# A gated mix of a long convolution and a two-layer network on one core: stage 2 of the convolution with taps and tokens in one product on 64x32 tiles, |C| in the exponent, a half-filled chunk of features packed into one operand

## The chip, the core and the metric

The kernel runs on one core of a Trainium2 chip. The core has a matrix engine (PE, TensorE) whose weight loads (PEld) are instructions of their own beside the matmuls, a vector engine (DVE, VectorE), an activation engine (ACT, ScalarE), a general engine (POOL, GpSimd) and an engine that here only issues transfers (SP, SyncE). Each engine works through its own list of instructions in a fixed order; semaphores hold an instruction back until what it reads is there. PE writes to PSUM, from where DVE and ACT read; POOL reaches only the large memory, SBUF. The metric is the time of one execution on the device in microseconds; several runs are taken, and the median counts.

## What is computed

Input u has 2048 tokens of 640 channels. `a` is a causal convolution of each channel with its own 2048 taps, which come from 128 complex modes; `b` is a two-layer network with 1728 hidden features; a sigmoid gate per token mixes them.

```python
dt = exp(log_dt)
A = -exp(log_A_real) + 1j * A_imag
C = (C_real + 1j * C_imag) * dt[:, None]
P = exp((A * dt[:, None])[:, :, None] * pos)          # pos = 0 .. 2047
K = 2.0 * einsum("dn,dnl->dl", C, P).real             # taps
a = irfft(rfft(u, 2 * L) * rfft(K, 2 * L))[:L] + u * D_skip
g = sigmoid((u * gate_w).sum(-1, keepdims=True))
b = relu(u @ w1) @ w2
out = g * a + (1 - g) * b
```

All inputs and the output are float32. The kernel splits the operands of the network into a high and a low part of a narrower format (f32r) and adds three products: high x high, high x low, low x high. The convolution's products stay in plain f32, and each such product stands in the profile as two MATMUL instructions.

## The kernel before

**A planner writes the order.** The kernel is written as tasks, each with an engine, a queue, an estimated duration, what it depends on and which buffers it takes or uses (`Plan.add`, L121). `Plan.run` (L160) plays the tasks through once, choosing on each engine the ready task of the best rank, and emits the instructions in that order. The order is fixed when the program is built; the chip then follows it, waiting where an estimate was too short. Tasks of one queue keep their order. Nearly every instruction bears line 228, where a helper records it, so the profile is read by tile names.

**The network (FFN), `feed_forward`, L278.** The 1728 features are cut into 14 chunks of 128, of which one has only 64; the chunks are worked in three passes (`PARTS`, 5, 5 and 4 chunks), each over 8 groups `g` of 256 tokens. The half-filled chunk stands first, in pass 0. `hidden` (L396) multiplies a pair of chunks with a group's tokens into the PSUM tile `pf`: 5 slices of 128 channels x 3 products per chunk, 256 columns each; ACT makes `hh` (ReLU, high part) and DVE `hl` (low part) from it. `sums` (L442) multiplies these with w2 into two halves of 320 columns for each of two blocks of 128 tokens, 3 products per chunk, and adds them to `q`, which is kept in DRAM between passes (`part`). In pass 0 the tokens are loaded (`xs`, L334, one buffer), turned by PE (`trans`, L343) and split into `xh` and `xl`. The 64 free feature columns of the half chunk hold zeros, save one that holds gate_w, so that the gate's logits come out of the hidden product as a row (`z`, L422) and go through DRAM to `gates` (L527). FFN tasks have the lowest rank on PE (5): they fill what the other work leaves.

**Parameters, `params`, L635.** Chains of DVE and ACT operations over 128x640 make the decay, the phase step, |C| and the angle of C. |C| takes a square root and a second set of five reciprocals. Rows of phase and decay go to DRAM (`ps`, L674) and are loaded back in another shape (`load_rows`, L798, 8 chunks of 16 channels at a time). |C| is turned by PE (`cm_pe`, L755) into the tile `cm`.

**Taps, `ssm`, L765.** 40 chunks of 16 channels. For each, PE expands phases (`pg`) and exponents (`px`, `pe`), ACT makes magnitudes (`mg`, `me`) by Exp and the trigonometric factors (`sn`, `cs`) by Sin, POOL multiplies `me` by `cm` (L862), and DVE forms five products (`factors`, L874). For each pair of chunks PE sums over the modes into `pk` (`taps`, L903), DVE turns that into `kt`, POOL adds D_skip, and the taps go to DRAM (`kd`).

**Convolution, `conv`, L960.** The transform over length is factored as 64 x 32. Five blocks `i` of 128 channels; for each block:

- `stage1` (L1014): PE transforms the 64-part for taps (from `ck`) and tokens (from `ut`), 4 quarters each; DVE turns the results into `vk` (taps, two buffers, one per block) and `va` (tokens, one buffer). Tokens of the next block wait for the relay of this one, since `va` is used again.
- `stage2` (L1044), 16 steps `j`: 12 products per step on 64x64 tiles, 128 columns each: one of the taps' spectrum and two of the tokens', the second with real and imaginary part exchanged. ACT copies the taps' part to `kw`, and one DVE multiply makes both halves of the complex product `t`.
- `inv2` (L1069), 8 steps: 16 products of 64 rows, which also add the halves of the complex product; ACT copies the result into `va`.
- `relay` (L1089): 8 DVE transposes from `va` into `vk`.
- `inv1` (L1096): 4 products with `tw`; the result is multiplied by the gate. Where the network's sum is already there, DVE multiplies and adds in one instruction (`join`, L1125) and the sum goes to the output; elsewhere ACT multiplies and the result goes to DRAM, to be added later (`with_y`, L495).

The convolution's PSUM tile `pc` has three buffers of two banks. On PE the ranks are 2 for stage 2 and its inverse, 3 for the first stages.

The heart of stage 2 and its inverse:

```python
for q, v, c0 in ((2, st['K', i], 0), (0, st['A'], 0), (1, st['A'], 32)):
    for e in range(2):
        for p in range(2):
            r, h = slice(p * 64, p * 64 + 64), p ^ e
            self.E.matmul(ps[h * 64:h * 64 + 64, p, q], st['tm'][r, 2 * j + e, c0:c0 + 64],
                          v[r, 2 * j + e], start=True, stop=True)
```

Of the kernel before, what the change touches and what calls it, by code (L numbers as in the profile page):

```python
# [24 lines left out]
SPIN = 10  # L25

# [10 lines left out]
def tables():  # L37
# [8 lines left out]
    m = np.zeros((2, 2, 32, 32, 3, 32))  # L46
    n = np.zeros((2, 2, 32, 32, 2, 2, 32))
    iw = np.zeros_like(w)
    for p in range(2):
        ct, st = c[p].transpose(2, 0, 1), s[p].transpose(2, 0, 1)  # L50
        m[p, 0, :, :, 0], m[p, 0, :, :, 1] = ct, st
        m[p, 1, :, :, 0], m[p, 1, :, :, 1] = -st, ct
        m[p, :, :, :, 2] = m[p, :, :, :, 0]
        for g in range(32):
            h = p ^ (g & 1)
            ck, sk = c[p, g], s[p, g]
            re, im = np.stack([ck, -sk], axis=1), np.stack([sk, ck], axis=1)
            n[h, 0, :, g, 0], n[h, 1, :, g, 0] = re, -re
            n[h, 0, :, g, 1], n[h, 1, :, g, 1] = im, im
            iw[p, :, g // 2 * 2 + h] = w[p, :, g]  # L60

    pt, mg, me = np.zeros((16, 8, 16, 64)), np.zeros((16, 8, 16, 64)), np.zeros((16, 8, 16, 32))
    for d in range(16):
        pt[d, :2, d, :32], pt[d, :2, d, 32:], pt[d, 2:4, d, :32] = b, 32 * b + 16, 1
        mg[d, 4:6, d], me[d, 4:6, d] = 32 * slots(), b
    tg = np.concatenate([x.reshape(128, -1) for x in (pt, mg, me)], axis=1)
    f = lambda x: np.ascontiguousarray(x.astype(np.float32))
    return dict(t_g=f(tg), t_f1=f(np.tile(np.stack([f1, f1[slots()]], axis=1), (2, 1, 1))), t_w=f(iw.reshape(128, 64)),
                t_m=f(m.reshape(128, 32, 96)), t_n=f(n.reshape(128, 32, 128)))
# [30 lines left out]
class Task:  # L100
    __slots__ = ('eng', 'q', 'dur', 'fn', 'deps', 'take', 'use', 'prio', 'mode', 'lag', 'end', 'kb', 'glue', 'port')


class Plan:
# [4 lines left out]
    HOLD = 0.3  # L109

# [10 lines left out]
    def add(self, eng, q, dur, fn, deps=(), take=(), use=(), rank=5, mode=None, kb=0, port=False):  # L121
        t = Task()
        t.eng, t.q, t.dur, t.fn, t.deps, t.take, t.use, t.mode = eng, q, dur, fn, tuple(deps), take, use, mode
        t.prio, t.end, t.kb, t.lag, t.glue, t.port = rank, None, kb, self.LAG[eng], [], port
        for b in (*take, *use):
            b.users += 1
            b.left += 1
# [15 lines left out]
    def ready(self, t, depth=0):  # L143
# [10 lines left out]
        for b in t.take:  # L154
            if not b.ring.slots:
                return 1e9, False
            r = max(r, min(b.ring.slots))
        return r, known

    def run(self):  # L160
        self.free = {e: 0.0 for e in self.LAG}
        mode, dma, log = {}, 0.0, []
        heads = {k: 0 for k in self.queues}
        while True:
# [36 lines left out]
            self.free[e] = start + change + t.dur  # L201
            if t.port:

                self.free[e] += min(max(self.free['POOL'] - start, 0), t.dur)
# [45 lines left out]
class Kernel:  # L250
    def __init__(self, tc, ctx, io, out):
# [8 lines left out]
                       xt=[T([2, 128, NT, 256], f"xt{g}") for g in range(8)], z=T([16, 128], "z_"),  # L260
                       part=[[T([128, 2, D], f"part{k}_{g}") for g in range(8)] for k in range(2)], y=T([128, 16, 4 * 128], "y_"))
        keep = self.keep = ctx.enter_context(tc.tile_pool(name="keep", bufs=1))
        self.gate, self.omg = keep.tile([128, 16], F32, name="gate"), keep.tile([128, 16], F32, name="omg")
        self.ident = keep.tile([128, 128], F32, name="ident")
# [13 lines left out]
    def feed_forward(self):  # L278
# [4 lines left out]
        for n, k in dict(ws=3, wq=5, xs=1, xhl=2, q=2, bank=2, z=1).items():  # L283
            ring(n, k)
# [12 lines left out]
        def weights(p, f, two, after=()):  # L297
            f0, fn = parts[p][f]
            first = p == 0 and not two
# [3 lines left out]
            def load():  # L303
                t = self.prm.tile([128, D], F32, name="wq", bufs=5) if first else pa.tile([128, D], F32, name="ws", bufs=3)
                st['ws', key] = t
                if two:
                    if fn < 128:
                        P.memset(t[fn:], 0.0)
                    D_.dma_start(t[:fn], io['B_w2'][f0:f0 + fn, :])
                    return  # L310
                t = t.rearrange("p (k f) -> p k f", f=128)
                if fn < 128:
                    P.memset(t[:, :, fn + 1:], 0.0)
                D_.dma_start(t[:, :, :fn], io['B_w1'][:, f0:f0 + fn].rearrange("(k p) f -> p k f", p=128))
                if fn < 128:
                    D_.dma_start(t[:, :, fn:fn + 1], io['gate_w'].rearrange("(k p o) -> p k o", p=128, o=1))

            def high():
                st[key] = [pa.tile([128, D], F32R, name=f"w{1 + two}{x}{f}") for x in 'hl']
                S.copy(st[key][0], st['ws', key])  # L320

            def low():
                V.tensor_sub(st[key][1], st.pop(('ws', key)), st[key][0].bitcast(F32))
# [10 lines left out]
        def load_x(g, after=()):  # L334
            s_ = tok('xs')

            def load():
                st['xs', g] = self.xp.tile([128, 2, D], F32, name="xs")
                for h in range(2):
                    D_.dma_start(st['xs', g][64 * h:64 * h + 64], xd[h, :, 2 * g:2 * g + 2, :])  # L340
            return s_, A('SP', 'x', 1.25, load, after, take=[s_], kb=640, rank=2 if g else 0)

        def trans(g, third, src):  # L343
# [34 lines left out]
            if third == 2:  # L378
                xst[g] = A('SP', 'st', 1.25, store, X[0, g], use=[x_], kb=1280, rank=6)
# [15 lines left out]

        def hidden(p, g, i, fs):  # L396
            b_, h_ = tok('bank'), tok(f"h{i}")

            def pe(r, f, third):
                def go():  # L400
# [3 lines left out]
                    wh, wl = (w.rearrange("p (k f) -> p k f", f=128) for w in (wh, wl))  # L404
                    for k in range(2 * third, min(2 * third + 2, NT)):
                        for m, (a, b) in enumerate(((wh, xh), (wh, xl), (wl, xh))):
                            self.E.matmul(st['hb'][:, r], a[:, k], b[:, k], start=k == m == 0,
                                          stop=k == NT - 1 and m == 2)
                return go
            ts = []  # L410
            for r, f in enumerate(fs):
                (wt, w_) = W[p, f, 0]
                for third in range(3):
                    x = X[p, g] if p else X[p, g][2 * third:2 * third + 2]
                    new = r == third == 0
                    ts.append(A('PE', 'ff', 0.72 if third < 2 else 0.36, pe(r, f, third), [*wt, *x],
                                take=[b_] if new else (), use=[w_, xtok[p, g]] + ([] if new else [b_]), mode='f'))

            if p == 0 and i == 0:
                z_ = tok('z')  # L420

                def zc():  # L422
                    st['z'] = pa.tile([65, 256], F32, name="z")
                    V.tensor_copy(st['z'][64:65], st['hb', i][64:65, 0])

                def zs():
                    D_.dma_start(sc['z'][2 * g:2 * g + 2], st['z'][64:65].rearrange("o (t p) -> o t p", t=2))
                zt = A('DVE', 'ff', 0.36, zc, ts, take=[z_], use=[b_], rank=0)
                self.zst.append(A('SP', 'st', 0.62, zs, [zt], use=[z_], kb=2, rank=6))

            def high():
                st['h', i] = [pa.tile([128, len(fs), 256], F32R, name=f"h{x}{i}") for x in 'hl']
                S.activation(st['h', i][0], st['hb', i][:, :len(fs)], AF.Relu)

            def low():
                V.scalar_tensor_tensor(st['h', i][1], st['hb', i][:, :len(fs)], 0.0, st['h', i][0].bitcast(F32),
                                       op0=ALU.max, op1=ALU.subtract)
            a = A('ACT', 'ff', 0.12 + 0.2 * len(fs), high, ts, take=[h_], use=[b_], rank=0)
            b = A('DVE', 'ff', 0.08 + 0.27 * len(fs), low, [a], use=[b_, h_], rank=0)
            H[p, g, i] = (a, b), h_  # L440

        def sums(p, g, j, q_, qld):  # L442
# [8 lines left out]
            prod = [(f, *x) for f in range(n) for x in ((0, 0), (0, 1), (1, 0))]  # L451
# [3 lines left out]
            def pe(ks):  # L455
                def go():
                    if ks[0] == 0:
                        st['sb', g, j] = pb.tile([128, 320], F32, name="pf")
                    for k in ks:
                        f, x, y = prod[k]  # L460
                        self.E.matmul(st['sb', g, j], st['h', f // 2 * 2][x][:, f % 2, ts_], st["w2", p, f][y][:, ns],
                                      start=k == 0, stop=k == 3 * n - 1)
# [14 lines left out]
            ks, a = list(range(3 * n)), []  # L477
            for k in range(0, 3 * n, 4 if j == 0 else 5):
                part = ks[k:k + (4 if j == 0 else 5)]
                dep = [x for f, _, y in (prod[k] for k in part) for x in W[p, f, 1][0]]  # L480
                dep += [hs[f // 2][0][x] for f, x, _ in (prod[k] for k in part)]
# [45 lines left out]
        def gates():  # L527
            def load():
                st['zt'] = pa.tile([128, 16], F32, name="zt")
                D_.dma_start(st['zt'], sc['z'].rearrange("b p -> p b"))  # L530

            def go():
                z = st['zt']
# [7 lines left out]
            a = A('SP', 'q', 0.62, load, self.zst, kb=8, rank=3)  # L541
            rec = Recorder(V)
            for k in range(17):
                a = A('DVE', 'gate', 0.2, rec.one(k, 17, go), [a], rank=4)
            self.gated = a

        self.zst, self.x_read = [], []
# [4 lines left out]
        if SPIN:  # L552
            A('PE', 'ff', 1.7 + 0.43 * SPIN, spin, mode='f')
        xs = {0: load_x(0)}
# [682 lines left out]
```

## Time and profile before

| | |
|---|---|
| median of 3 runs | 714.4 us (713.83 to 715.64) |
| the profiled execution | 717.8 us, of which 716.0 are the span from the first to the last instruction |
| mean granted clock of PE | 0.986 |
| instructions | 21643, of which 9489 matmuls and as many weight loads |

A row of a group in the profile gives line, engine, operation, output tile <- input tiles, shape and count; then busy time in all and the mean of one in ns; then how long the engine stood idle just before them, and what ended it. Matmuls overlap in time, so their mean is a latency: what one costs is read from the distance of their starts. "issue" as a reason for a wait means that the engine waited for nothing that the profile shows. In rows of stretches, each engine's busy time is followed by its count of instructions, then PE's granted clock, the share of the transfer engines and GB/s.

### The profile page before, as it was taken

What the parts mean: (1) busy time and instruction counts of PE and PEld (TensorE: products, weight loads), DVE (VectorE), ACT (ScalarE), POOL (GpSimd) and SP (SyncE); (2) the same over time, 40 slices, a digit from 0 to 9 for tenths busy, and PEclk for the clock granted to TensorE, in tenths of its full rate; (3) what the DMA queues carried; (4) which work ended last, traced back from release to release, by engine and by line L of the source; (5) the groups of instructions that cost most, each with busy time, mean ns of one, the idle gap of its engine ahead of it and who ended that gap; (6) DMA issues with size and microseconds to landing.
All of it is one profiled execution on the core that took longest, in us unless ns stands there. A gap on an engine that the chain in (4) does not pass through costs nothing.

```text
span 716.0 us, 21643 instructions
## 1 busy us (share of the span) xinstructions
PE 679.6 (95%) x9489; PEld 600.1 (84%) x9489; DVE 575.4 (80%) x833; ACT 389.2 (54%) x572; POOL 72.2 (10%) x81
## 2 busy tenths in 40 slices
PE   5979999999999999999999999989999999899897
PEld 5979998898999999989998897886587776597695
DVE  4499628988999999999999986649869769479675
ACT  4353339999998778787889820151340531241330
POOL 1000002211121221112211100000000000010020
PEclk9899999999999999999999999999999999899999
DMA  9844773254467334423432759924915914731534
GB/s 219 242 193 163 260 240 111 67 179 163 138 199 248 125 124 139 160 88 103 153 108 89 226 166 303 270 93 137 199 44 170 251 56 119 177 97 61 120 98 96
DMA packets 92167, 110.84 MB, mean 155 GB/s; under 512 B 30945, under 2 KB 73705, under 8 KB 91817
## 3 DMA queue, kind: packets, MB, share of 16 engines
q1 hardware_dynamic: 91992, 109.38, 51.9%
q8 instruction: 74, 1.21, 0.7%
q14 instruction: 21, 0.16, 0.1%
q10 hardware_dynamic: 80, 0.08, 0.0%
HBM read 70.24 MB, written 39.20 MB: 153 GB/s over the span
## 4 chain that ended last, share of the span: by engine, by line
PE 69%; DVE 14%; ACT 10%; issue 4%; DMA 2%; SPq 1%; DVEq 0%; ACTq 0%
PE pf L228 40%; PE pc L228 21%; PE pk L228 4%; DVE sn L228 3%; ACT cs L228 3%; DVE G L228 2%; DVE mg L228 2%; ACT sn L228 2%; PE pg L228 2%; ACT L228 1%; PE px L228 1%; DMA xs<-in_A_u_dram 1%; SPq L228 1%; ACT hh L228 1%; DVE cs L228 1%
## 5 line engine op out<-in xcount | busy, mean ns | idle before, releaser
L228 PE MATMUL pf<-xh,w1h 128*128 128x256 f32 x560 | 165.0, 295 | 0.6 <-ACT xh L228 0.6
L228 PE MATMUL pf<-xl,w1h 128*128 128x256 f32 x560 | 159.9, 286 | 0.6 <-DVE xl L228 0.6
L228 PE MATMUL pf<-xh,w1l 128*128 128x256 f32 x560 | 159.5, 285 | 0.0
L228 PE MATMUL pf<-w2h,hh 128*128 128x320 f32 x448 | 140.0, 315 | 2.8 <-DVE hl L228 2.0
L228 PE MATMUL pf<-w2l,hh 128*128 128x320 f32 x448 | 137.6, 310 | 0.0
L228 PEld LDWEIGHTS pf<-xh,w1h 128*128 128x128 f32 x560 | 108.5, 194 | 22.9 <-issue 20.0
L228 PE MATMUL pf<-w2h,hl 128*128 128x320 f32 x448 | 126.4, 311 | 0.5 <-DVE hl L228 0.5
L228 ACT ACTIVATE hh<-pf 128x512 fp32r<-128x512 f32 (+1 forms) x64 | 34.7, 543 | 149.3 <-PE pf L228 142.4
L228 PEld LDWEIGHTS pf<-xl,w1h 128*128 128x128 f32 x560 | 108.5, 194 | 1.8 <-DVE xl L228 0.8
L228 PEld LDWEIGHTS pf<-xh,w1l 128*128 128x128 f32 x560 | 108.5, 194 | 0.0
L228 DVE TENSOR_TENSOR t<-pc,kw 128x512 f32<-128x512 f32 x80 | 53.9, 691 | 50.3 <-ACT kw L228 50.2
L228 PEld LDWEIGHTS pf<-w2h,hh 128*128 128x128 f32 x448 | 84.1, 188 | 11.6 <-issue 5.9
L228 PEld LDWEIGHTS pf<-w2l,hh 128*128 128x128 f32 x448 | 84.2, 188 | 2.4 <-issue 1.6
L228 PEld LDWEIGHTS pf<-w2h,hl 128*128 128x128 f32 x448 | 80.8, 188 | 6.3 <-issue 4.6
L228 POOL TENSOR_TENSOR me<-me,cm 128x512 f32<-128x512 f32 x40 | 51.5, 1287 | 192.7 <-DVE cs L228 115.2
L228 DVE TENSOR_TENSOR mg<-mg,cs 128x1024 f32<-128x1024 f32 x40 | 56.4, 1409 | 1.3
L228 PE MATMUL pc<-va,tm 64*64 64x128 f32 x1280 | 55.3, 277 | 1.9 <-issue 1.9
L228 DVE TENSOR_TENSOR sn<-pg,cs 128x1024 f32<-128x1024 f32 x40 | 48.7, 1216 | 8.6 <-ACT cs L228 8.3
L228 ACT ACT_TABLE_LOAD x42 | 53.9, 1283 | 0.7
L228 ACT CAST cs<-pg 128x1024 int32<-128x1024 f32 x40 | 40.4, 1011 | 20.0 <-PE pg L228 19.8
L228 DVE STREAM_TRANSPOSE vk<-va 128x512 f32<-128x512 f32 x40 | 46.9, 1233 | 4.2 <-ACT va L228 4.2
L228 DVE SCALAR_TENSOR_TENSOR hl<-pf,hh 128x512 fp32r<-128x512 f32 (+1 forms) x64 | 39.3, 616 | 12.3 <-ACT hh L228 11.8
(140 smaller groups left out, 1218.9 us busy)
## 6 DMA issues: line engine op xcount, KB each, us to landing
part<-q SPq DMA_DIRECT2D x16, 640.0 KB, 3.8
xh<-xt SPq DMA_DIRECT2D x16, 640.0 KB, 4.5
xl<-xt SPq DMA_DIRECT2D x16, 640.0 KB, 7.1
q<-part SPq DMA_DIRECT2D x16, 640.0 KB, 4.0
ws<-in_B_w_dram SPq DMA_DIRECT2D x22, 320.0 KB, 3.9
xs<-in_A_u_dram SPq DMA_DIRECT2D x16, 320.0 KB, 4.0
xt<-xh SPq DMA_DIRECT2D x8, 640.0 KB
xt<-xl SPq DMA_DIRECT2D x8, 640.0 KB
```

What stands on the lines that cost most here:

```text
L228: return lambda *a, **k: self._tc.keep_in_program_order(f(*a, **k))
```

## The change

In the convolution:

- `vk` and `va` become one tile `ku` of two halves, two buffers, so that taps and tokens of a group lie side by side. Tokens of the next block no longer wait for the relay.
- `stage2` has 8 steps of 16 products on 64x32 tiles, each of 256 columns (taps and tokens together); the product with exchanged parts is gone. ACT copies the taps' half of the result (real and imaginary part) over the taps in `ku`; two DVE multiplies take it with the tokens' imaginary part (into the new tile `kx`, three buffers) and with their real part (in place), reading the tokens from PSUM; POOL subtracts and adds the partial products.
- `inv2` has 2 steps of 64 products of 32 rows on 32x64 tiles; the first is put behind step 6 of stage 2 (`LATE`). Each takes two of the three `pc` buffers; ACT copies out.
- `inv1`: ACT multiplies everything by the gate; where the network's sum is there, POOL adds it. New tile `yo` for all, `yj` for the loaded sums.
- ranks change; the tables `tm` and `tn` shrink.

In the taps and parameters: ln|C| is made from the exponent and mantissa bits of the larger part of C and an Ln, joins the rows in DRAM as a fourth set, and is added by PE in the exponent; `cm`, its transposes and POOL's product are gone. The square root and its five reciprocals go. Rows are loaded for 4 chunks at a time. The phase rows are split and stored before the decay is computed.

In the network: high and low part of the half chunk's w1 stand side by side in one operand, so two products do for three; ACT and DVE fold the two halves of the result. w2's 64 rows are loaded twice. The logits are made by DVE from the loaded tokens (`logits`, two instructions per group) with gate_w broadcast to all partitions; the way through DRAM goes. `xs` has two buffers.

In the planner: every 128 matmuls (a block of PE's instructions) are held to start at least 3.6 us apart, and a buffer can be taken twice by one task.

```diff
             if e == 'PE':
+                done += t.n
+                while done >= 128:
+                    done -= 128
+                    at = self.free[e] - t.dur * done / t.n
+                    self.free[e] += max(0, block + self.FETCH - at)
+                    block = max(at, block + self.FETCH)
...
+        def logits(g):
+            def go(t):
+                x = st['xs', g][:, t]
+                V.scalar_tensor_tensor(x, x, 1.0, self.gw, op0=ALU.mult, op1=ALU.mult,
+                                       accum_out=self.z[:, 2 * g + t:2 * g + t + 1])
...
+                    ms = ((wh, xh), (wh, xl), (wl, xh))[:2 if halves(p, f) else 3]
-                        for m, (a, b) in enumerate(((wh, xh), (wh, xl), (wl, xh))):
+                        for m, (a, b) in enumerate(ms):
...
+            if lo:
+                x = A('ACT', 'ff', 0.32, fold, ts, take=[z_], use=[b_], rank=0)
+                x = A('DVE', 'ff', 0.35, total, [x], use=[b_, z_], rank=0)
+                x = A('ACT', 'ff', 0.32, half_high, [x, a], use=[z_, h_], rank=0)
+                x = A('DVE', 'ff', 0.35, half_low, [x], use=[z_, h_], rank=0)
...
-            prod = [(f, *x) for f in range(n) for x in ((0, 0), (0, 1), (1, 0))]
+            prod = [(f, *x) for f in range(n) for x in ((0, 0), (0, 1), (1, 0))[:2 if halves(p, f) else 3]]
...
-            e = A('POOL', 'g2', 1.2, lambda: P.tensor_mul(st['me', c], st['me', c], self.cm[:, c * C:c * C + C, None]
-                                                          .to_broadcast([128, C, 32])), [b, self.cm_done], use=[m_])
...
         def stage2(i, j, dep):
+                ps = self.psc.tile([128, 2, 4, C], F32, name="pc")
+                for a in range(2):
+                    for m in range(4):
                         for p in range(2):
+                            r, g = slice(p * 64, p * 64 + 64), 4 * j + m
+                            self.E.matmul(ps[32 * m:32 * m + 32, p, 2 * a:2 * a + 2], st['tm'][r, g, 32 * a:32 * a + 32],
+                                          st['ku', i][r, :, g], start=True, stop=True)
+                st['p2', i, j] = ps.rearrange("q p (a k) c -> q k a p c", a=2)
             def copy():
+                S.copy(whole(i, j), st['p2', i, j][:, 0])
+            def mul(a):
+                def go():
+                    k = whole(i, j)
+                    if a:
+                        st['kx', i, j] = self.pr.tile([128, 2, 2, C], F32, name="kx", bufs=KX)
+                    V.tensor_mul(st['kx', i, j] if a else k, st['p2', i, j][:, 1, None, a].to_broadcast([128, 2, 2, C]), k)
+                return go
+            def add(k):
+                def go():
+                    y, x = whole(i, j)[:, k], st['kx', i, j][:, 1 - k]
+                    (P.tensor_add if k else P.tensor_sub)(y, y, x)
+                return go
...
+        def inv2(i, h, dep):
+            bs = tok('psc'), tok('psc')
+                for g in range(4):
                     for q in range(2):
+                        for m in range(4):
                             for p in range(2):
+                                r = slice(32 * m, 32 * m + 32)
+                                self.E.matmul(px[m // 2][p * 64:p * 64 + 64, m % 2, g], st['tn'][r, 4 * h + g, p, q],
+                                              whole(i, 4 * h + g)[r, q, p], start=q == 0, stop=q == 1)
...
+                def join(b0=b0, ns=ns):
+                    y = st['yo', i, b0][:, :ns]
+                    P.tensor_add(y, y, st['yj', i, b0][:, :ns])
```

More of the change, by code (lines that the diff above doesn't have):

```diff
@@ L25 @@
 SPIN = 10
+S4R = 3
+SKR = 3
+SUR = 3
+SKD = 3
+SUD = 1
+LATE = 3
+KX = 3
+XS = 2
+POOLED = 0
+PA = 4
+PL = 2.5
+RL = 'dve'
+YO = 2
+YJ = 2
+KRANK = 3
 def slots():
@@ L153, in ready @@
                 r = max(r, d.end - d.lag if d.eng == t.eng else d.end)
[L154 to L155 removed]
+        for b in set(b.ring for b in t.take):
+            k = sum(x.ring is b for x in t.take)
+            if len(b.slots) < k:
                 return 1e9, False
[L157 removed]
+            r = max(r, sorted(b.slots)[k - 1])
         return r, known
@@ L298, in weights @@
             f0, fn = parts[p][f]
-            first = p == 0 and not two
+            first, half = p == 0 and not two, fn < 128 and not two
             s_, w_ = tok('wq' if first else 'ws'), tok(f"w{1 + two}{f}")
@@ L751, in params @@
                                   [a], use=[s_], rank=4))
[L753 to L763 removed]
+        return [*done, *self.tg_done]
     def ssm(self, C=16):
@@ new lines, in inv1, with store @@
+                a = A('PE', 's4', 0.87, pe, [*dep, tw], take=[b_], use=[K[i]], rank=S4R, mode='c1')
+                c = A('ACT', 's4', 1.12, copy, [a], take=[x for x in (y_, g_ if first else None) if x],
+                      use=[b_] + ([g_] if g_ and not first else []), rank=1)
+                self.need_gates.append(c)
+                if ns < 4:
+                    if not last:
+                        def store(b0=b0, ns=ns):
+                            D_.dma_start(self.sc['y'][:, b0 + ns:b0 + 4, i * C:i * C + C], st['yo', i, b0][:, ns:])
+                        c2 = A('SP', 'y4', 0.62, store, [c], use=[y_], kb=64 * (4 - ns), rank=4)
+                    self.y_st[i, b0 // 4] = c if last else c2
@@ L1165, in conv @@
+                    ld = A('SP', 'yq', 0.62 * ((ns + 1) // 2), load, [opened], take=[j_] if new else (), use=() if new else [j_],
+                           kb=64 * ns, rank=3)
+                    self.need_sums.append((ld, [(b0 + b) // 2 for b in range(0, ns, 2)]))
+                    own = A('POOL', 's4', 0.1 + 0.25 * ns, join, [c, ld], use=[y_, j_], rank=2)
+                    A('SP', 'y4', 1.25, out, [own], use=[y_], kb=64 * ns, rank=4)
         self.y_st, self.need_sums, self.need_gates, self.gy_tok = {}, [], [], None
```

416 lines of the change are left out of this document (201 added, 215 removed).

## The prediction

> **What bounds the kernel now.** I read the page's busy line first, then busy time by stage, then the chain of work that ended last, then groups of instructions.
>
> ```profile
> PE 679.6 (95%) x9489; PEld 600.1 (84%) x9489; DVE 575.4 (80%) x833; ACT 389.2 (54%) x572; POOL 72.2 (10%) x81
> ```
>
> The stages are the making of the taps (106 to 432 us), the convolution (432 to 684) and the tail. In each row come the stretch, its length, then busy time of PE, PEld, DVE, ACT and POOL:
>
> ```profile
> 106.00:432.00 326.00, 317.81 (x4460) 298.71 (x4459) 302.27 (x418) 270.70 (x323) 60.22 (x60) 1.00 0.45 144
> 432.00:684.00 252.00, 241.33 (x4052) 186.35 (x4054) 187.43 (x258) 72.68 (x165) 5.01 (x7) 0.98 0.56 149
> 684.00:716.00 32.00, 27.73 (x332) 23.75 (x324) 20.77 (x36) 5.52 (x12) 5.14 (x6) 1.00 0.38 87
> ```
>
> PE is busy 97% of the first stage and 96% of the second. FFN products fill whatever the other work leaves free, and every product has to be done before the end. So the end is set by the sum of PE's work, and a PE microsecond removed counts wherever it lies, as long as FFN work is left to move into it. DVE is at 93% in the first stage and 74% in the second: it is the next bound.
>
> What a product costs I take from uninterrupted pieces of the chain (start, length, what, count):
>
> ```profile
> 85.60 3.60 PE pf L228 x30
> ...
> 91.70 8.81 PE pf L228 x60
> ...
> 146.42 1.97 PE pk L228 x128
> ...
> 460.95 6.79 PE pc L228 x227
> 467.74 2.36 issue
> ...
> 516.70 9.73 PE pc L228 x337
> ...
> 565.28 7.14 PE pc L228 x254
> 572.42 1.68 issue
> ...
> 674.62 8.11 PE pc L228 x274
> ```
>
> A hidden product of 256 columns takes 3.60/30 = 0.120 us, an output product of 320 columns 8.81/60 = 0.147. The four dense stretches of stage 2 and inverse stage 2 hold 227+337+254+274 = 1092 matmuls in 35.81 us with their "issue" waits: **32.8 ns each**. The array itself needs less, as two neighbours of the timeline show:
>
> ```profile
> 463.76 1.05 PE L228 MATMUL pc<-t,tn 64*64 64x128 f32 x32
> 464.63 0.40 PE L228 MATMUL pc<-vk,tm 64*64 64x128 f32 x8
> ```
>
> 32 matmuls start within 0.87 us: 27.2 ns each. The rest is instruction supply: PE waits for "issue" after dense bursts of 227 and 254 matmuls.
>
> ```profile
> q8 instruction: 74, 1.21, 0.7%
> ```
>
> 74 packets carry PE's 18,978 instructions (9489 matmuls and as many weight loads), 256 to a packet, 128 matmuls. A burst of 128 (the taps' row at 146.42) runs at 1.97/128 = 15.4 ns, so supply allows that for one packet, and stalls after about two.
>
> **The change part by part.** Groups on which it bears (count, busy, mean ns):
>
> ```profile
> L228 DVE TENSOR_TENSOR mg<-mg,cs 128x1024 f32<-128x1024 f32 x40 | 56.4, 1409 | 1.3
> L228 PE MATMUL pc<-va,tm 64*64 64x128 f32 x1280 | 55.3, 277 | 1.9 <-issue 1.9
> L228 DVE TENSOR_TENSOR t<-pc,kw 128x512 f32<-128x512 f32 x80 | 53.9, 691 | 50.3 <-ACT kw L228 50.2
> ...
> L228 PE MATMUL pc<-t,tn 64*64 64x128 f32 x1280 | 47.3, 278 | 1.5 <-DVE t L228 1.2 <-issue 0.2
> ```
>
> *Stage 2 on PE.* Two of three products here are the tokens' (the row with 1280 instructions), one the taps': 5 blocks x 16 x 12 products, two instructions each, make 1920 of 128 columns. They become 5 blocks x 8 x 16 products, two instructions each: 1280 of 256 columns. Twice the columns on eight tiles instead of four gives the old 27.2 ns of array per instruction, if eight run at once. I charge the dense 32.8 ns: 640 fewer save **21.0 us** (17.4 at the array's rate).
>
> *Inverse stage 2 on PE.* Still 1280 instructions, now 32 rows deep on eight tiles: half the array time, 13.6 ns. The saving lies between nothing (supply bound at 32.8) and 1280 x (32.8-15.4) = 22.3 us. The nearest row is the taps' 128 in 1.97, the same burst; but here two bursts follow stage 2. Stage 2 itself will be slowed by its multiplies (below), so supply can catch up before. I take 256 x 17.4 ns = 4.5 us a block less one "issue" wait of 2.0 (between 1.68 and 2.36): 2.4 a block, **12 us**. The Trainium skill, "Runtime: NRT & Kernel Launch", Instruction fetch mechanics, says that crossing a block of 256 instructions is mostly hidden. By that rule the saving would be 22 us; the two waits above contradict it.
>
> *FFN.* The chunk of 64 features takes two products instead of three: 8 groups x 5 = 40 hidden (4.8 us) and 8 x 4 = 32 output products (4.7): **9.5 us**, all in pass 0. In exchange each group gets two small ACT and two small DVE operations in a row before the first output product. Cover: the other two pairs' hidden products of that group, 45 x 0.120 = 5.4 us. Without it about 2 us per group (estimate of 0.5 each, between 0.336 for 128 columns and 0.691 for 512 in rows below and above), 16 in all.
>
> *Visits.* Stage 2 gets gaps on PE that FFN will fill, and each return to stage 2 costs:
>
> ```profile
> 614.38 0.86 PE pc L228 x24
> ```
>
> 0.86 against 24 x 27.2 = 0.65: 0.2 us. Six more per block: **+6 us** (0 to 12).
>
> *Chain inside a block.* Stage 2 was PE, ACT copy, DVE multiply. Now PE, ACT copy, two DVE multiplies of the same 128x512 form (0.69 each, 80 in all as before), two adds on POOL, inverse stage 2. The adds have 256 elements:
>
> ```profile
> L228 POOL TENSOR_TENSOR q<-q,ws 128x256 f32<-128x256 f32 x2 | 1.4, 725 | 52.2 <-ACT kw L228 52.2
> ```
>
> 16 x 0.725 = 11.6 us a block on an engine that used 5 us in the whole stage; 16 x 0.69 = 11.1 on DVE beside it. With inverse stage 2 (4 to 7) and its copies this is about 18 us a block; before, 640 x 32.8 = 21. Queued behind an add are POOL's joins of y and later adds, and inverse stage 2 waits for them. The other DVE work of a block is
>
> ```profile
> L228 DVE STREAM_TRANSPOSE vk<-va 128x512 f32<-128x512 f32 x8 | 9.3, 1236 | 1.9 <-ACT va L228 1.9
> L228 DVE STREAM_TRANSPOSE vk<-pc 128x512 f32<-128x512 f32 x8 | 7.8, 1047 | 0.0
> L228 DVE STREAM_TRANSPOSE va<-pc 128x512 f32<-128x512 f32 x8 | 7.4, 1043 | 0.0
> ```
>
> 24.5 us, of which the token transposes (7.4) no longer wait for the previous block's relay, since U has two buffers. 24.5+11.1 is 36 of a block's 52.6 us (three blocks lie between the starts at 516.70 and 674.62), so DVE has room. Cost 0, cover: FFN products; without it, see the first rival. The Trainium skill, "Perfetto Trace Analysis", Optimizing Scalar/DVE Operations, says GpSimd and DVE share an SBUF read port, so moving work between them may not help. The trace agrees where both inputs lie in SBUF (mg, below); stage 2's multiplies read one from PSUM. If they were held by each add too, DVE would take up to 11.6 us more a block, which is the first rival.
>
> *Joins of y.*
>
> ```profile
> L228 DVE SCALAR_TENSOR_TENSOR yj<-pc,gate,yj 128x128 f32<-128x128 f32 x36 | 10.0, 336 | 1.7 <-DMA yj<-part 1.0 <-ACT yj L228 0.4 <-PE pc L228 0.3
> ```
>
> These leave DVE for ACT and POOL, 29% and 2% busy in that stage: 0, with 10 us of DVE freed.
>
> *Taps.* |C| goes into the exponent, so 40 POOL products go. They are off the path, but stretch what DVE does beside them, as the chain shows against POOL's timeline:
>
> ```profile
> 167.03 1.96 DVE mg L228
> ...
> 202.33 1.23 DVE mg L228
> ```
>
> ```profile
> 166.40 1.50 POOL L228 TENSOR_TENSOR me<-me,cm 128x512 f32<-128x512 f32 x1
> ```
>
> The same multiply takes 1.96 us beside POOL and 1.23 without; by the mean of 1.409 that is 40 x 0.18 = 7 us of DVE's 302. Against it 16 logits of 640 elements on DVE (estimate 0.8 each from 0.691 for 512) put 13 us in, over half of it before 106. Both lie beside PE's work: 0 (-8 to +6). The parameter chain, the second set of exponents and the order of its stores move DVE work before 106, where FFN covers: 0 (-5 to +5). The five transposes of |C| leave PE, each of 128 columns and so below a hidden product's 0.120: -0.5.
>
> *Start.* The first 18 us (last number: GB/s moved) and a row of the timeline:
>
> ```profile
> 0.00:18.00 18.00, 10.25 (x61) 9.38 (x61) 8.85 (x14) 8.71 (x14) 1.81 (x9) 0.98 0.96 219
> ```
>
> ```profile
> 17.99 1.08 PE L228 MATMUL pk<-ident,xs 128*128 128x128 f32 x4 [4.67 <-DMA xs<-in_A_u_dram]
> ```
>
> PE waits 4.67 us for the second tile of x, which is queued behind the weights. The broadcast gate weights (320 KB) and a second copy of 64 rows of w2 (160 KB) go in ahead of it on SP's queue; at 219 GB/s that is 2.2 us. The gate's column load (2.5 KB) goes. The second x buffer doesn't help here, since SP issues x behind the weights either way. **+2 us** (0 to 4).
>
> **Sum**: -21.0 -12 -9.5 +6 -0.5 +2 = -35.0. Against the profiled execution of 717.8 us (span 716.0 and 1.8 around it) that is 682.8; the median of the runs is 714.4, 3.4 lower, so **679.4 us**. Bounds of the terms (inverse stage 2 from 0 to 22, visits, taps, start) give 665 to 697.
>
> **Rivals.** (1) *The block's chain becomes the bound.* The convolution stays near 252 us because POOL's adds, DVE's multiplies and the relay follow one another and PE's freed time stays empty but for FFN drawn out of the tail:
>
> ```profile
> 684.00:716.00 32.00, 18.82 (x132) 17.78 (x132) 5.46 (x10) 1.20 (x2) 1.00 0.38 87
> ```
>
> (the tail's row of FFN tiles alone: 18.8 us of PE). Half of it drawn in, with the FFN's 9.5: 714.4-9.5-0.5+2-9.4 = 697. For it: 11.6 us on POOL in line; against: DVE's third of free time in the stage. (2) *Supply never stalls*, as the page has it: inverse stage 2 saves 22, visits cost nothing: 663. Against it speak the two waits. (3) *Slower: eight tiles don't run at once, only four.* No row shows 64x32 or 32x64 tiles. Then stage 2 takes 1280 x 54.4 ns = 69.6 us instead of 1920 x 32.8 = 63.0, inverse stage 2 saves nothing, and the sum is +6.6 -9.5 -0.5 +6 +2 = +4.6: 719. It decides from 51 ns per instruction. For it: nothing; against: 64x64 tiles take 4 x 27.2 = 109 ns for 128 columns of f32 (two instructions each), near the 120 of one full FFN product with 256 columns, so four do run at once. This is also the case in which the change doesn't do what it says.
>
> **How the numbers follow.** Forecast, 0.60: 679, own range 666 to 692. Rival 1, 0.19: 692 to 710. Rival 2, 0.12: 657 to 667. Rival 3 and other losses of the block's chain, 0.09, of which 0.03 within 0.3% (about what a measurement of this kernel can tell from no change, 2 us) and 0.06 above. Faster 0.91. The range 661 to 705 leaves out 0.05 of rival 2, 0.04 of rival 1, and rival 3: 0.18.
>
> **What would show it.** Stage 2's rows with 1280 instructions of 64x256 starting 27 ns apart (51 or more is rival 3); inverse bursts of 128 in about 2 us, with "issue" waits behind them or not (rival 2); FFN pieces between stage 2's; the convolution shortened to some 225 us; PE still over 93% there, otherwise rival 1, with PE waiting on POOL. The FFN groups 40 and 32 instructions fewer. It would be wrong if PE's sum fell as said while its idle time grew as much.

## The result, and the profile after

The changed kernel takes **693.5 us** (median of 4 runs, 692.3 to 695.6) against 714.7 for the kernel before in the same job: ratio 0.971, interval 0.9686 to 0.9734. The forecast was 679.4 with a range of 661 to 705; the time lies in the range, 14 us above the forecast and just outside the part of the range that the prediction gave to the forecast, 666 to 692. The profiled run spans 692.3 us.

The busy line of the page of the changed kernel:

```profile
PE 641.4 (93%) x8772; PEld 541.9 (78%) x8772; DVE 554.7 (80%) x821; ACT 396.9 (57%) x579; POOL 91.9 (13%) x133
```

PE's busy time fell from 679.6 to 641.4, by 38.2 us; the PE terms of the forecast add up to 37. But span less busy time was 36.4 us and is 50.9: 14.5 us of the saving came back as idle PE. The stages in windows (stretch, length, busy time of PE, PEld, DVE, ACT, POOL, clock, DMA share, GB/s): start, taps, convolution from its first to its last product, tail.

```profile
0.00:108.00 108.00, 90.58 (x646) 88.80 (x647) 70.77 (x146) 44.78 (x86) 0.87 (x7) 0.94 0.75 224
108.00:421.00 313.00, 306.65 (x4360) 286.74 (x4359) 287.66 (x428) 267.88 (x323) 8.51 (x20) 1.00 0.44 144
421.00:670.00 249.00, 225.92 (x3639) 148.59 (x3637) 191.57 (x240) 80.78 (x160) 77.10 (x100) 0.98 0.59 154
670.00:692.30 22.30, 18.29 (x134) 17.76 (x132) 4.69 (x8) 3.48 (x10) 5.46 (x7) 1.00 0.41 90
```

The taps went from 326 to 313 us; DVE, which had 302 us to do there, has 288. In the prediction the convolution's stretch, 432 to 684, ends ahead of its last products. From the first to the last, and behind that, the kernel before has

```profile
434.00:705.40 271.40, 260.43 (x4320) 202.34 (x4318) 203.68 (x283) 77.57 (x174) 9.27 (x10) 0.98 0.54 141
705.40:716.00 10.60, 6.63 (x44) 5.87 (x40) 3.96 (x11) 0.62 (x2) 0.88 (x2) 1.00 0.70 150
```

So the convolution, with the FFN work inside it, went from 271.4 to 249.0 us, while PE's idle time in it rose from 271.4 - 260.4 = 11.0 to 249.0 - 225.9 = 23.1 us. And FFN work is left over: 18 us of PE in the last stretch, where it was 6.6. The chain of work that ended last shows how it comes to lie there (start, length, what):

```profile
657.24 6.52 DVE ku L249 x6
663.76 0.04 issue
663.80 6.27 PE pc L249 x16
670.07 10.93 PE pf L249 x84
...
681.67 6.73 PE pf L249 x44
```

PE waits for the last relays on DVE, finishes the last block, and only then runs FFN products that could have filled its gaps. What PE waited for in the convolution (window 421 to 670; total us, times, longest):

```profile
PE pc L249 <- DVE ku L249: 13.7, 17, 4.2
PE pc L249 <- issue: 4.7, 6, 1.5
```

The relays and stage 1's transposes on DVE, not POOL's adds, are what PE waits for. The pieces of stage 2 and its inverse themselves, on PE's timeline:

```profile
491.20 1.96 PE L249 MATMUL pc<-ku,tm 64*32 64x256 f32 x64
...
494.01 1.96 PE L249 MATMUL pc<-ku,tm 64*32 64x256 f32 x64
...
498.86 2.10 PE L249 MATMUL pc<-ku,tn 32*64 32x128 f32 x128
500.88 1.09 PE L249 MATMUL pc<-ku,tm 64*32 64x256 f32 x32
...
506.42 1.86 PE L249 MATMUL pc<-ku,tn 32*64 32x128 f32 x111
509.74 0.54 PE L249 MATMUL pc<-ku,tn 32*64 32x128 f32 x17 [1.46 <-issue]
```

64 instructions of 256 columns take 1.96 us and 32 take 1.09: 0.87 us for 32 more, 27 ns each. A burst of 128 inverse instructions starts at 498.86 and the next piece at 500.88: 15.8 ns each. The second burst stalls on supply after 111.

### The profile page after: what moved, and what is told of

Read it like the earlier page. It is cut to its first block, busy times and chain, and to the rows that moved or that the text cites. A ratio compares the mean times of both kernels' runs of the same rounds, so it can differ in the third digit from the quotient of the medians.

```text
span 692.3 us, 20324 instructions
## 1 busy us (share of the span) xinstructions
PE 641.4 (93%) x8772; PEld 541.9 (78%) x8772; DVE 554.7 (80%) x821; ACT 396.9 (57%) x579; POOL 91.9 (13%) x133
## 5 line engine op out<-in xcount | busy, mean ns | idle before, releaser
L249 PE MATMUL pf<-xh,w1l 128*128 128x256 f32 x520 | 148.1, 285 | 0.6 <-DVE w1l L249 0.6
L249 PE MATMUL pf<-w2h,hl 128*128 128x320 f32 x416 | 118.4, 314 | 0.6 <-DVE hl L249 0.5
L249 PEld LDWEIGHTS pf<-xh,w1l 128*128 128x128 f32 x520 | 100.5, 193 | 0.8 <-DVE w1l L249 0.8
L249 PEld LDWEIGHTS pf<-w2h,hl 128*128 128x128 f32 x416 | 75.0, 188 | 6.2 <-issue 3.3
L249 ACT COPY ku<-pc 128x512 f32<-128x512 f32 (+1 forms) x60 | 42.0, 733 | 65.1 <-PE pc L249 65.1
L249 DVE STREAM_TRANSPOSE ku<-pc 128x512 f32<-128x512 f32 x80 | 75.4, 1073 | 3.9 <-PE pc L249 3.9
L249 POOL TENSOR_TENSOR ku<-ku,kx 128x256 f32<-128x256 f32 x80 | 56.2, 734 | 103.2 <-DVE ku L249 55.8
L249 POOL TENSOR_TENSOR kt<-kt,dsk 128x8 f32<-128x8 f32 x20 | 8.5, 426 | 403.3 <-DVE kt L249 403.3
L249 DVE STREAM_TRANSPOSE ku<-ku 128x512 f32<-128x512 f32 x40 | 46.8, 1239 | 8.8 <-issue 5.5
L249 DVE TENSOR_TENSOR mg<-mg,cs 128x1024 f32<-128x1024 f32 x40 | 48.9, 1223 | 1.5
```

Of the source, the lines that this page charges most:

```text
L249: return lambda *a, **k: self._tc.keep_in_program_order(f(*a, **k))
```

## The experiments

All of them are edits of the changed kernel; times are medians, ratios are to the kernel before on the same chip. Five theories are named in the expectations. A: FFN can't fill PE's gaps since both pf banks are held by sums that wait for y. B: the order of the two inverse bursts makes a block's chain longer than needed. C: DVE's serial work of a block (transposes, relays, multiplies) sets when PE goes on. D: instruction supply takes what the waits on DVE give up. E: PE's order was planned with durations that are too short.

**e1, y behind the sums.** In the last pass groups 3 to 6 leave PSUM first; POOL adds y afterwards.

```diff
+            if g > YLATE:                  # YLATE = 6
+                for t in range(2):
+                    ts[t] += join(t, ts[t])
...
                     es = [sums(p, g, j, q_, mx[t]) for j in (2 * t, 2 * t + 1)]
+                    if g <= YLATE:
+                        es += self.join_y[g](t, es)
```

> Edit: in the last FFN pass, groups 3 to 6 take their sums out of PSUM first and add y behind them; before, the DVE's q waited for the POOL's q<-q,ws. Theory A (FFN can't fill the convolution's gaps because both pf banks are held by sums whose q waits for y): PE's idle time in the convolution falls from 23 us to about 12, the FFN work behind the last pc from 17.8 to about 7, and the time by 4 to 6 us, to 687.5-689.5. Theory B (the block's own chain is the bound, FFN has nothing to do with it): idle time and time unchanged within 1 us.

Measured 694.0 us, ratio 0.9704 (0.9657 to 0.9751): no change. But inside much of what theory A says did happen. The waits in the same window, and the window behind the last pc:

```profile
PE pc L250 <- issue: 10.9, 9, 3.3
PE pc L250 <- DVE ku L250: 3.2, 10, 0.8
```

```profile
678.50:693.60 15.10, 8.47 (x55) 7.40 (x51) 2.90 (x5) 3.20 (x11) 4.77 (x6) 0.95 0.49 104
```

The waits on DVE fell from 13.7 to 3.2 us and PE's work in the tail from 18.3 to 8.5; the waits for issue rose from 4.7 to 10.9, and the convolution's end moved from 670 to 678.5, since FFN work moved into it. PE's idle time there fell only to 18.6 us where A had about 12, and 2.6 us of this came back in the tail (6.6 us of idle PE, 4.0 before). A is a true cause of waits, but alone it buys nothing.

**e2, the first inverse burst last.**

```diff
-LATE = 3
+LATE = 4
```

> Edit: LATE 3 -> 4, the first inverse burst goes behind all eight pieces of stage 2 instead of ahead of the eighth, so that two bursts of 128 follow each other. Theory B (the block's chain bounds: the eighth piece with its copy, two multiplies and two adds came late because the burst was put ahead of it): 5 to 7 us faster, 686.5-688.5, idle in the convolution 23 -> about 14. Theory A: within 1 us. Theory D (instruction supply): 256 dense matmuls in a row wait longer for issue, 26 us of PEld issue waits grow by 1 to 2 us a block, time up by 0 to 8 us.

Measured 693.0 us, ratio 0.9698 (0.9639 to 0.9757): no change that can be told.

```profile
PE pc L249 <- issue: 8.1, 5, 2.6
PE pc L249 <- DVE ku L249: 7.4, 14, 2.1
```

Again the waits on DVE fall (13.7 to 7.4) and those for issue rise (4.7 to 8.1), now with both bursts behind each other. That is D's picture, and B's gain was given back.

**e3, both.**

> Both edits of e1 and e2. If A and B are two causes, they add: 9 to 13 us faster than the changed kernel, 681-685. If they open the same gaps, it is no better than the better of the two by more than 2 us.

Measured **688.3 us**, ratio 0.9632 (0.9581 to 0.9683), 5 us below the changed kernel: better than either, short of the sum of what A and B had promised. The waits, and PE's timeline at one burst and at a later one:

```profile
PE pc L250 <- issue: 8.4, 7, 2.7
PE pc L250 <- DVE ku L250: 2.9, 9, 0.5
```

```profile
481.40 1.32 PE L250 MATMUL pc<-ku,tn 32*64 32x128 f32 x69
485.45 2.00 PE L250 MATMUL pc<-ku,tn 32*64 32x128 f32 x59 [2.72 <-issue]
...
596.53 2.05 PE L250 MATMUL pc<-ku,tn 32*64 32x128 f32 x123
600.78 0.53 PE L250 MATMUL pc<-ku,tn 32*64 32x128 f32 x5 [2.20 <-issue]
```

DVE is nearly out of PE's way, and PE stops in the middle of bursts for instructions.

What "issue" is in these rows can be told by counting in the trace. Counted together from the start, PE's matmuls, weight loads and semaphore instructions reach the same place of a block, 193 past a multiple of 256, at each of e3's five longest waits for issue (0.8 to 2.7 us), and each of these waits ends 1.2 to 1.6 us after a packet of the instruction queue (q8) has landed. By this mark supply stops PE in the convolution for 5.2 us in the changed kernel, 9.6 in e1, 8.6 in e2 and 9.0 in e3.

**e12, FFN ahead of a piece that supply would stop.** e3, with a choice in the planner, which already kept a count of packets (`done`, `block`, 3.6 us each):

```diff
+                    if t.n >= 20:
+                        n2, f2 = done + t.n, start + t.dur
+                        late = 0
+                        if n2 >= 128:
+                            n2 -= 128
+                            late = block + self.FETCH - (f2 - t.dur * n2 / t.n)
+                        if late > 0.5:
+                            for r2, t2 in c:
+                                if t2.q == 'ff' and r2 <= at + 0.1:
+                                    t, start = t2, max(at, r2)
```

The choice holds for every PE task of 20 or more matmuls, so for the taps' sums too.

> Edit: e3, and the planner puts a ready FFN piece ahead of a piece of stage 2 or a burst that would run into instruction supply by over 0.5 us. Against e3 (688.3; bursts waiting 8.7 us for issue): theory D (what the waits on DVE give up, supply takes): the bursts' issue waits fall and it is 2 to 5 us faster than e3, 683-686. If supply's waits don't count: the same as e3 within 1.5 us.

Measured **681.6 us** (681.1 to 681.9), ratio 0.9532 (0.9492 to 0.9571): 12 us below the changed kernel with the same work on every engine. The waits and the window of its convolution:

```profile
PE pc L260 <- issue: 5.5, 4, 3.0
PE pc L260 <- DVE ku L260: 3.3, 8, 1.4
```

```profile
422.00:664.50 242.50, 230.07 (x3690) 155.47 (x3688) 193.87 (x243) 81.25 (x161) 77.90 (x101) 0.99 0.61 159
```

Both waits are low at once, and PE is idle for 12.4 us of the convolution, near the 11.0 of the kernel before. The gain over e3, 6.7 us by the medians and 5.5 by the spans (685.6 and 680.1), is more than D had expected (2 to 5). Of it, 2.9 us are waits of pc for issue; the rest I can't put to one row. So D is shown for about half of the step, and whether another order would give as much is not tried.

**e11, the planner's durations.** Seven kinds of convolution tasks get what the trace shows, for instance:

```diff
-            return A('DVE', 'rl', 1.14, ...
+            return A('DVE', 'rl', 1.24, ...
```

> Edit: the planner gets the durations that the trace of the changed kernel shows for the seven kinds of conv tasks that it has too short (multiply 0.68, add 0.73, relay 1.24, transpose 1.07, copies 0.59 and 1.03, burst 2.02); only orders change. Rival theory E (PE waits since its order was planned with too short durations): PE's waits on DVE in the convolution, 20 us, fall by half, 5 to 8 us faster, 685.5-688.5. Theory C (the waits are DVE's work itself, whatever the order): within 2 us of 693.5.

Measured 692.4 us, ratio 0.9682 (0.9642 to 0.9723): 1 us, within the uncertainty.

```profile
PE pc L249 <- issue: 13.5, 7, 5.4
PE pc L249 <- DVE ku L249: 2.7, 9, 0.7
```

By this list the waits on DVE are gone and "issue" has grown. But the two longest pauses, 4.2 and 5.4 us ahead of stage 1's pieces, are not supply. The timeline of the first, on PE and on DVE:

```profile
524.95 1.98 PE L249 MATMUL pc<-ck,tf 64*64 64x512 f32 x8 [4.24 <-issue]
514.20 8.89 DVE L249 STREAM_TRANSPOSE ku<-ku 128x512 f32<-128x512 f32 x8 [0.28 <-issue]
522.96 1.89 DVE L249 STREAM_TRANSPOSE ku<-pc 128x512 f32<-128x512 f32 x2
```

PE goes on 0.1 us after DVE has turned the piece of stage 1 before (522.96 + 1.89 = 524.85), which had stood behind the relays. The second pause is the same: transposes from 616.33 to 618.23, PE goes on at 618.33. Neither lies at the place of a block where supply stops PE, and no packet of instructions landed in the 8 us before they ended. So the two belong to DVE, whose waits are then 2.7 + 4.2 + 5.4 = 12.3 us, hardly less than 13.7; supply takes 2.4. The longer durations moved these waits and did not remove them, as C says; E is wrong.

**e6, half a relay.** Each relay on DVE moves 8 of its 16 columns; half of the relayed spectrum is left out, all orders stay.

```diff
-            d = slice(r * 16, r * 16 + 16)
+            d = slice(r * 16, r * 16 + 8)
```

> Edit: each of the 40 relays on DVE (ku<-ku, 1.24 us) transposes 8 of its 16 columns; the other half of the relayed spectrum is left out. The order of every engine stays. DVE has 25 us less to do in the convolution. Theory C (DVE's serial work of a block, transposes and relays, sets when PE's next pieces may start): PE's waits on DVE ku fall, 6 to 11 us faster, 682-688. Theories A and B alone (pf banks, order of the bursts): within 1.5 us of 693.5.

Measured 684.2 us, ratio 0.9563 (0.9521 to 0.9605): 9 us faster. The convolution's window:

```profile
421.00:657.00 236.00, 220.19 (x3633) 146.51 (x3632) 171.38 (x238) 80.64 (x160) 72.11 (x96) 1.00 0.60 158
```

DVE has 20 us less to do (191.6 to 171.4), the stretch is 13 us shorter, and PE's waits on DVE ku go from 13.7 to 8.1. Of the 13 us, 7.3 are idle time of PE (23.1 to 15.8); the other 5.7 are its own work (225.9 to 220.2), at a granted clock of 1.00 instead of 0.98. As C says, 20 us of DVE are worth 9 of time in the order as it was planned, though DVE is busy for only 77% of that stage.

**e9 and e7, POOL's adds taken away and doubled.** In e9 an add works on 8 of 256 elements, the rest of that sum is left out; in e7 a multiply by ones of the same shape goes ahead of each. All other orders stay.

```diff
+                    y, x = y[:, :, :4], x[:, :, :4]                                          # e9
+                    P.tensor_mul(z, z, self.ones[:, None, None].to_broadcast([128, 2, 4, 32])) # e7, z is y
                     (P.tensor_add if k else P.tensor_sub)(y, y, x)
```

> Edit: the 80 POOL adds of stage 2 work on 8 of their 256 elements; the rest of the complex product's sum is left out. No engine's order changes. POOL's part of a block's chain goes from 11.7 us to 2 or 3. By e7 (12.4 us more a block cost 7.3 us) on a straight line the adds themselves cost 5 x 9 x 0.6 = 27 us; by theory C (DVE's serial work bounds, POOL's adds only just don't) 1 to 5 us: 688-692. By the forecast's step (covered): within 1.5 us of 693.5.

> Edit: ahead of each of the 80 POOL adds of stage 2 a POOL multiply of the same 128x256 elements by ones; no other engine's order changes. POOL's part of a block's chain goes from 11.7 to about 24 us. The forecast's step (chain at no cost, covered by FFN products): within 2 us of 693.5. If the chain is not covered: slower by most of 5 x 12 = 60 us less what FFN pieces still fill, 710 to 730.

e9 took 693.8 us, ratio 0.9703 (0.966 to 0.9747): nothing gained. e7 took 730.2, ratio 1.0204 (1.0151 to 1.0257): 37 us lost. Their windows of the convolution, e9 first:

```profile
422.90:669.00 246.10, 223.77 (x3633) 146.91 (x3632) 191.11 (x240) 80.69 (x160) 35.11 (x100) 0.99 0.59 155
```

```profile
422.00:709.00 287.00, 242.87 (x3637) 155.53 (x3636) 194.02 (x240) 81.23 (x160) 134.66 (x180) 0.92 0.51 133
```

With 42 us less on POOL the stretch is 3 us shorter; with 58 more it is 38 longer. The adds, 80 x 0.73 / 5 = 11.7 us a block, are hidden; at twice that two thirds of the excess show. Of the 38 us, 21 are idle time of PE (23.1 to 44.1) and 17 the same work of PE taking longer (225.9 to 242.9), at a granted clock of 0.92 instead of 0.98. A cost of nothing here was no slack to rely on.

**e4, the half chunk's third products.** 72 products with a stationary operand of zeros, in their old places.

```diff
+                            if halves(p, f) and m == 0:
+                                self.E.matmul(st['hb'][:, r], self.zero, xh[:, k], start=False, stop=False)
...
+                        if y and halves(p, f):
+                            self.E.matmul(st['sb', g, j], self.zero, st["w2", p, f][y][:, ns], start=False, stop=False)
```

> Edit: 72 products (40 hidden, 32 output) with a stationary operand of zeros put back into the half chunk, in the same places of the same order; no other engine's order changes. The forecast's step (PE's work counts one for one, 40 x 0.120 + 32 x 0.147 = 9.5 us): +9.5 us, about 703. If PE's idle time in pass 0 takes them up: 0 to +4, 693.5-697.5.

Measured 706.4 us, ratio 0.9881 (0.9818 to 0.9945): 13 us slower by the medians, with 4 us of uncertainty; by the spans 701.4 - 692.3 = 9.1, of a profiled run that was the fastest of its four (703.2 to 711.0). The forecast's 9.5 lies within the uncertainty, 0 to 4 does not: FFN work on PE counts in full, even in a kernel that has 23 us of idle PE elsewhere.

**e5, the old convolution in the changed kernel.** The `conv` method of the kernel before and its tables; half chunk, |C|, logits and planner stay as changed.

> Edit: the convolution of the kernel before (1920 instructions of stage 2 with 128 columns, 64x64 inverse tiles, y joined on DVE) with its tables, in the changed kernel; half chunk, |C| in the exponent, logits on DVE and the start stay. By the forecast's terms for the convolution (-21 -12 +6) it is 27 us slower than the changed kernel, about 720. If the convolution's saving on PE was half lost to new waits (PE's work there fell by 37 us, its time beside work rose by 13), it is 12 to 16 us slower: 705-710.

Measured 715.5 us (709 to 718 over ten runs), ratio 0.9998 (0.9965 to 1.0032). The new convolution is worth 715.5 - 693.5 = 22 us by the medians and 712.2 - 692.3 = 19.9 by the spans, neither 27 nor 12 to 16; all other parts together nothing by the medians (2.4 us of uncertainty) and 3.8 us by the spans (716.0 - 712.2). Its convolution's window has PE idle for 11.0 us:

```profile
419.50:701.00 281.50, 270.51 (x4383) 210.33 (x4382) 206.09 (x288) 80.26 (x178) 9.29 (x10) 0.98 0.56 145
```

So the idle time of the changed kernel came with the new convolution and not with the FFN or the taps.

**e8, a POOL product back in the taps.**

```diff
+            def pooled():
+                me = st['me', c]
+                P.tensor_mul(me, me, self.ones[:, None].to_broadcast([128, C, 32]))
...
+            b = A('POOL', 'pm', 1.5, pooled, [b], use=[m_])
```

> Edit: the 40 POOL products of the taps are back, as multiplies of me by ones of the same 128x512 elements, planned with 1.5 us as before; |C| stays in the exponent. DVE's mg multiplies go back from 1.22 to about 1.41 us. The forecast's step (taps: 0, beside PE's work, -8 to +6): within 3 us of 693.5, the taps longer by 7 and the rest shorter. If the taps are bound by DVE and FFN can't move: +7 to +15, 700-709.

Measured 711.8 us, ratio 0.9965 (0.9934 to 0.9995): 18 us slower, more than either expectation. The group of DVE's mg multiplies and the window of the taps:

```profile
L249 DVE TENSOR_TENSOR mg<-mg,cs 128x1024 f32<-128x1024 f32 x40 | 57.3, 1432 | 1.9 <-ACT q L249 0.5
```

```profile
109.00:443.00 334.00, 313.11 (x4391) 291.62 (x4393) 307.33 (x431) 271.84 (x327) 71.97 (x60) 0.99 0.43 138
```

The multiply is back at the 1.4 us of the kernel before, DVE has 20 us more, the stage is 21 us longer and PE idle for 20.9 us in it. The longest list of waits there is PE's pg for DVE's sn: 11.2 us, 1.4 in the changed kernel. The changed planner charges a quarter of the time beside POOL where the old one charged all of it, so this order was made for a DVE that is faster than the chip's. What the product cost in the kernel before, under its own planner, e8 does not settle; the total that e5 gives for all parts but the convolution, 0 to 3.8 us with the FFN's products in it, leaves little room for it.

**e10, no gate weights.** The 320 KB aren't loaded and POOL fills their tile, so that the gate is computed from other logits.

```diff
-            D_.dma_start(self.gw, io['gate_w'].rearrange("(o d) -> o d", o=1).to_broadcast([128, D]))
+            P.memset(self.gw, 0.01)
```

> Edit: the gate weights aren't loaded (320 KB ahead of x on SP's queue); POOL fills their tile with a constant, so the gate is computed from other logits. All orders stay. If the start's loss is this transfer: PE's wait for the second tile of x goes from 6.9 to about 4.7 us, the second wait (for xl on DVE, 6.4) stays, and the kernel is 2 to 3 us faster, 690.5-691.5. If the transfer is hidden behind the weights: no difference.

Measured 690.4 us, ratio 0.9659 (0.9611 to 0.9707); this interval still touches that of the changed kernel, but the wait doesn't leave a doubt. PE's two longest waits of the start in the changed kernel, then in e10:

```profile
20.58 1.08 PE L249 MATMUL pk<-ident,xs 128*128 128x128 f32 x4 [6.93 <-DMA xs<-in_A_u_dram]
```

```profile
PE pk L249 <- DVE xl L249: 7.2, 2, 6.5
PE pk L249 <- DMA xs<-in_A_u_dram: 4.5, 2, 4.1
```

The wait for x is 4.1 without the transfer, 6.9 with it and was 4.67 before the change. The second wait, for xl, is 6.4 to 6.5 in both and was 4.8; the logits now stand in DVE's queue at that place, which I haven't tried apart.

## Why the prediction was right, and where it failed

The time lies in the stated range only by way of rival 1's share of it, 692 to 705.

**What bounds the kernel.** Right: PE's work counts (e4). That PE's sum fell by 38 where 37 were forecast is in part luck: against e5's trace the convolution's work on PE fell by 31.5 us (27 forecast), that of all other parts by 6.7 (10 forecast). The prediction's sign of being wrong, idle time that grows as much as PE's sum falls, came to 14.5 of 38.2 us.

**Stage 2 on PE, -21.** Right in kind: 27 ns for twice the columns, so eight 64x32 tiles run at once. Rival 3 is out; it needed 51.

**Inverse stage 2, -12.** Right in kind: 128 instructions take 2.0 us, and a second burst meets supply (1.46 us at 509.74). Rival 2, no stalls, is out. By the array's rates alone the two stages saved 640 x 27.2 ns = 17.4 and 1280 x (27.2 - 15.8) = 14.6, together 32 us.

The prediction set the second burst's stalls against the Trainium skill, "Runtime: NRT & Kernel Launch", Instruction fetch mechanics, by which crossing a block of 256 instructions is mostly hidden. That does not fit a stretch in which 128 matmuls with their weight loads take 2.0 us: the trace's records of the instruction queue have packets of one block starting at 482.7, 487.2 and 490.8 in e3, and PE stopped for 2.72 us at 482.7. For the size of PE's instruction memory that section has both 2048 instructions and two blocks. The trace fits the two: from 478.0 to the stop PE ran 205 matmuls with their weight loads, 1.6 blocks, and no packet started between 472.1 and 482.7.

**Visits, +6.** Too large. In the traces PE comes to stage 2 or its inverse from other work 26 times, and 18 times before the change: 8 visits more, not 30, or 1.6 us at the prediction's 0.2.

**FFN, -9.5.** Right: 40 and 32 products gone, 9.1 by the spans of e4 and 13 by its medians, with 4 of uncertainty.

**Chain inside a block, cost 0, "cover: FFN products".** This step failed. From e5 to the changed kernel PE's busy time falls by 31.5 us (672.9 to 641.4), but its idle time rises by 11.6 (39.3 to 50.9), so that 19.9 came out. The text had put the danger on POOL and cleared it: rightly for POOL, as e9 shows, but PE waits on DVE, which the forecast took to have "room" from its 36 busy of 52.6 us a block. Room over a block isn't room in a chain: transposes, multiplies and relays come one behind the other on DVE, stage 2 of a block needs the transposes, which can stand behind the relays of the block before (as at 514.20 in e11), and e6 gives 9 us for 20 us of relays. And the cover was no cover, for two reasons that follow each other. FFN pieces weren't ready when PE had gaps (e1: banks behind y), and where they or a better order did close these gaps, stage 2 came so dense that supply stopped it. Two different edits (e1, e2) took much of the waits on DVE away, supply took 4.4 and 3.4 us more, and the time stayed where it was; a third (e11) only moved the waits on DVE. Both edits together gave 5 us, and with FFN pieces set between dense pieces as well (e12) the time went to 681.6, 2 us from the forecast. Its sum was that of an order which the changed kernel doesn't have.

So rival 1 was half of what happened: its sign, PE under 93% in the convolution, came (225.9 of 249.0 is 91%), and 693.5 lies in its range, but not by its mechanism; the convolution did get shorter, and PE waited on DVE and not on POOL.

**Start, +2.** Right in cause, too small: the wait for x grew by 2.3 us (4.67 to 6.93), and the second wait, on DVE, by another 1.6.

**Taps, 0.** The stage did get shorter with DVE's work, as much as DVE lost, and its FFN work moved on; e5 finds no net gain there. That it is free in either direction is not so: e8 lost 18 us.

By the spans the 14.1 us between forecast and result are 7.1 in the convolution (27 forecast, 19.9), 4.2 in all other parts (8 forecast, 3.8; of this 2 in the start, 2 not found), and 2.8 from setting spans against medians: the span before lay 1.6 above the median of the runs (716.0 and 714.4), the one after 1.2 below it (692.3 and 693.5).

## What to carry to other kernels

When a filler is to cover a chain, ask at each gap whether a filler piece is ready there: its banks, its own inputs and its place in a fixed order decide, not its total. An engine that is busy for three quarters of a stage can still be what everything waits for, if its pieces lie in line. And where matmuls get shorter than the rate at which instructions arrive, spread them among long ones: an order that closes the other waits but runs short pieces back to back gives part of its gain back.

## What the runs showed that I had not expected

- Waits change hands without the time changing: between 421 and 670 us the sum of PE's waits of pc on DVE and issue is 14.1 us in e1 and 15.5 in e2, 18.4 in the changed kernel, and the times lie within 0.5 us of it. e12 has 8.8. And a wait that the list puts under "issue" can be one on an engine: e11's two longest end with DVE's transposes.
- A link that costs nothing can be close to the edge: taking 42 us of POOL's work away gave nothing, adding 58 cost 37.
- The granted clock moves, but not with the total of PE's idle time alone: in the convolution it is 0.98 in the changed kernel with 23 of 249 us idle, 0.92 in e7 with 44 of 287, 1.00 in e6 with 16 of 236, yet 0.98 in the kernel before with 11 of 271. The Trainium skill, "TensorE: Matmul & The Clock Gate", Part 1, has the clock go down after an idle window of about 3.4 us; the start of the changed kernel agrees, with 0.21 us from product to product behind the wait of 6.93 us and 0.12 again from 24.0 on.
